# The turn between forward and backward of a decode block on one core: norms' sums gathered, do from a transposed Wo, loads and stores around it reordered

## The chip, the cores and the metric

The kernel runs on one core of one Trainium2 chip. The time is the device time of one execution in microseconds (us). The kernel before takes 1381.98 us, the median of 3 runs (1381.88 to 1382.74). A profiled execution gives, for each engine, what ran when and what it waited for. The engines are PE (matrix products), DVE (vector), ACT (scalar functions), POOL (here it only issues stores) and SP (issues loads); all transfers run on the core's 16 DMA engines.

## The reference

Forward and gradients of one block for a single token. Attention reads a cache of 32 heads, 8192 positions, 192 columns, in bf16; the gradients for K and V have the same size, so the kernel reads and writes some 570 MB.

```
h  = layernorm(x) * (1 + ca) + sa              # sa, ca, ga, sb, cb, gb from silu(c) @ w_mod
q  = h @ wq;  p = softmax(q k^T / sqrt(192));  o = p v
x  = x + ga * (o @ wo)
hb = layernorm(x) * (1 + cb) + sb
x1 = hb + (terms that shift one token, which are zero here)
x  = x + gb * (x1 + gelu(layernorm(x1) @ w3) @ w4)
grads with respect to x, k_cache, v_cache, wq, wo, w3, w4, c, w_mod
```

With p the softmax of a head and do the gradient that reaches its o: dV = p (outer) do, dP = V do, dS = p * (dP - p.dP), dK = dS (outer) q.

## The kernel before, in words

**Vectors as columns.** A vector of 640 is kept as a tile of 128 partitions by 5 columns. A layer norm needs sums over all of it: DVE adds along the columns, PE multiplies with a constant matrix (`negd_mat`, all -1/640, or `ones_mat_f`), which sums over the partitions and leaves the result on every one, and DVE goes on from PSUM. `ln_cols` (L152) does this twice, for the mean and then for the variance; `ln_bwd_cols` (L172) once.

**Forward.** For each head, K and V come in two tiles of 128 x 32 x 192 (1536 KB each). DVE multiplies K with q (L131, `prod`), PE adds up the scores (L359), ACT and DVE scale K by the exponentials (L392, L400, tile `EK`, four quarters a head) and PE makes products of V with the scaled K (L417 and L425, `fwd_kvA` and `fwd_kvB`, into banks A and B of PSUM) and the sum of the scaled K (L433, `fwd_kvK`, into `kb_ps`). The last column of `EK` carries the exponentials alone, so that the same product gives o. `fwd_keep` and `fwd_keepB` bring these banks to SBUF for the backward.

**The turn.** After head 31: o of the last pair, its product with Wo (L488), x1, the two norms, u = n2 @ w3 (L751), the gelu and its derivative, dn2 = du @ w3^T (L792), two norms backward, dao, do of the last pair (L1111), and do broadcast to all partitions (L190, `do_pb`). Only then can a dV be made. Beside it PE transposes w3 (60 blocks in 15 groups of 4, L646, with a cast by ACT each, L647) and the last pair's rows of Wo (L655), DVE makes the gradient of w4 (`dw4_some`, L782, with stores at L785) and the sums `d_g` (L524), and the four `fwd_kvK` of head 31 run.

**Backward.** Heads go from 31 down to 0. `bwd_dv` writes one dV tile: of its 32 rows ACT makes 20 (L948) and DVE 12 (L915), and POOL issues the store (L954). `bwd_mult` multiplies a V tile by do in place (L131), and PE adds it up (L930), which frees its slot for the next load. `bwd_dk` makes dK (DVE, L915; store at L969).

**Order.** The code's order is each engine's order: `pin_order` fixes it for PE, DVE and ACT, and SP and POOL issue in the order written, so an issue that waits for a slot holds back those behind it. V tiles in the backward, and batches of Wo, come through a ring of six slots (`ring_load`), of which a slot is loaded again when the tile in it is used up. K tiles, the weights w3 and w4 (`w_t`) and the output tiles share the pool `big` of five slots.

Of the kernel before, what the change touches and what calls it, by code (L numbers as in the profile page):

```python
# [20 lines left out]
def kernel(  # L21
# [43 lines left out]
    P = 128  # L65
# [75 lines left out]

    def col_sums(parts, n, name):
        ps = bank_c(name)
        nc.tensor.matmul(ps[:, 0:n], lhsT=ones_mat_f, rhs=parts, start=True, stop=True)
        return ps[:, 0:n]
# [6 lines left out]
    def ln_cols(x_c, pfx, fill=lambda k: None):  # L152
# [3 lines left out]
        fill(0)  # L156
# [4 lines left out]
        nc.vector.tensor_tensor_reduce(out=sq, in0=xc, in1=xc, scale=1.0 / D, scalar=0.0, op0=ALU.mult, op1=ALU.add, accum_out=s2)  # L161
# [5 lines left out]
        fill(1)  # L167
        nrm = ccol(NDC, pfx + "_n")
        nc.vector.tensor_scalar(out=nrm, in0=xc, scalar1=rstd[:, 0:1], scalar2=None, op0=ALU.mult)
        return nrm, rstd  # L170

    def ln_bwd_cols(dn, n, rstd, add_to, out, pfx, fill=lambda: None):  # L172
        s = ccol(2, pfx + "_s")
        nc.vector.reduce_sum(out=s[:, 0:1], in_=dn, axis=AX.X)
        jk = ccol(NDC, pfx + "_jk")
        nc.vector.tensor_tensor_reduce(out=jk, in0=dn, in1=n, scale=1.0, scalar=0.0, op0=ALU.mult, op1=ALU.add, accum_out=s[:, 1:2])
        m_ps = neg_means(s, 2, pfx + "_m")
        fill()
        t = ccol(NDC, pfx + "_t")
        mul(t, n, m_ps[:, 1:2].to_broadcast([P, NDC]))  # L180
        add(t, t, dn)
        add(t, t, m_ps[:, 0:1].to_broadcast([P, NDC]))
        stt(out, t, rstd[:, 0:1], add_to, ALU.mult, ALU.add)
# [54 lines left out]
    fpr_cm = tc.tile_pool(name="fprod", bufs=2)  # L238
    fpr = fpr_cm.__enter__()
# [36 lines left out]
    n0_c, r0 = ln_cols(x0_c, "ln0")  # L276
# [48 lines left out]

    def load_v(pool, h, t):
        tl = pool.tile([P, JH, DH], BF16, name="V_sb")
        nc.sync.dma_start(out=tl, in_=V_hd[h][:, t * JH : (t + 1) * JH, :])
        return tl
# [14 lines left out]
    def fwd_mult(h, t, st):  # L344
# [3 lines left out]
        prod = fpr.tile([P, JH, DH], BF16, name="prod")  # L348
# [126 lines left out]

    def fwd_o(hp):
        c0 = 3 * hp
        for h in (2 * hp, 2 * hp + 1):
            _, _, bp, ca_, cb_ = head_split(h)
            mul(o_col_f[:, ca_ : ca_ + 1], MA(h)[:, DH : DH + 1], rinv_bc[:, h : h + 1])  # L480
            mul(o_col_f[bp : bp + 64, cb_ : cb_ + 1], MB(hp)[bp : bp + 64, DH : DH + 1], rinv_bc[bp : bp + 64, h : h + 1])
        dve_copy(o_col_bf[:, c0 : c0 + 3], o_col_f[:, c0 : c0 + 3])
# [7 lines left out]
    def fwd_ao_add(hp, sm):  # L490
        if hp == 0:
            dve_copy(ao_c, sm[:, 408 : 408 + NDC])
        else:
            add(ao_c, ao_c, sm[:, 408 : 408 + NDC])

# [14 lines left out]

    def load_wt(k):
        w_t.append(flat(big_tile(f"w_t{k}")))
# [7 lines left out]
    def dg_some(f0, f1):  # L520
        jk_t = fpr.tile([P, JH, DH], BF16, name="prod").rearrange("p j d -> p (j d)")
        for f in range(f0, f1):
            jk = jk_t[:, f % 4 * D : (f % 4 + 1) * D]
            nc.vector.tensor_tensor_reduce(out=jk, in0=w4n(f, 0, D), in1=dbo_bc, scale=1.0, scalar=0.0, op0=ALU.mult, op1=ALU.add, accum_out=d_g[:, f : f + 1])  # L524
# [36 lines left out]
    for i in range(1, HQ + 2):  # L561
        if i == HQ + 1:
            nc.scalar.activation(out=warm, in_=eps_c, func=ACT.Sqrt)
# [6 lines left out]
        if i == HQ - 1:  # L570
            load_wt(0)
        fwd_load(i - 1, 1)
        if p:
            fwd_wo(i - 1, st[i - 1])
        if i == HQ:
            load_wt(1)
            load_wt(2)
        if pp:
# [6 lines left out]
        if i % 2 == 0 and i >= 4:  # L585
            fwd_ao((i - 4) // 2, st[i - 3]["wo"], st[i - 1]["sm"])
            fwd_ao_add((i - 4) // 2, st[i - 1]["sm"])
        if pp:
# [3 lines left out]
        if i > HQ:  # L592
            dg_some(9, NFC)
# [33 lines left out]
        if i == HQ:  # L627
            dg_some(0, 9)
    SB = [1024]
# [9 lines left out]
    w3T_next = [0]  # L639

    def w3T_some(n):
        for g in range(w3T_next[0], min(w3T_next[0] + n, NFC * NDC // 4)):
            t_ps = bank("s", 2, "t_ps", SB[0])
# [3 lines left out]
            nc.scalar.copy(out=w3T(4 * g, 4), in_=t_ps[:, 0:512])  # L647
        w3T_next[0] += n

    def woT_some(n):  # L650
        for g in range(woT_next[0], min(woT_next[0] + n, 4)):
            t_ps = bank("s", 2, "t_ps", SB[0])
            blks = range(4 * g, min(4 * g + 4, 3 * NDC))
            for k, blk in enumerate(blks):
                nc.tensor.matmul(t_ps[:, k * P : (k + 1) * P], lhsT=woT[:, blk * P : (blk + 1) * P], rhs=ident_bf, start=True, stop=True)  # L655
            nc.scalar.copy(out=woT[:, 512 * g : 512 * g + P * len(blks)], in_=t_ps[:, 0 : P * len(blks)])
        woT_next[0] += n

    woT = st[HQ - 1]["wo"].rearrange("p c r -> p (c r)")
    woT_next = [0]  # L660
    w3T_some(3)
    fwd_kvK(HQ - 1, 0, st[HQ - 1], True)
    fwd_kvK(HQ - 1, 1, st[HQ - 1], True)
    sm = bank_c("sm_ps")
    fwd_ao(HH - 1, st[HQ - 1]["wo"], sm)
    fwd_ao_add(HH - 1, sm)
    fwd_kvK(HQ - 1, 2, st[HQ - 1], True)
# [3 lines left out]
    fpr_cm.__exit__(None, None, None)  # L671
    psum_cm.__exit__(None, None, None)
    psum[0] = ctx.enter_context(tc.tile_pool(name="psum_b", bufs=1, space=bass.MemoryType.PSUM, reuse_waits="tile"))
    CB[0], SB[0] = 2, 512

    bv = ctx.enter_context(tc.tile_pool(name="bv", bufs=3, reuse_waits="tile"))
# [5 lines left out]
    V_b = {HS[0]: st[HS[0]]["V"]}  # L682
# [10 lines left out]
    def ring_load():  # L693
        while ring_n[0] < len(ring) and (ring_n[0] < NR - 2 or ring_key(ring_n[0] - NR) in freed):
            kind, k, t = ring[ring_n[0]]
            pool = bv if ring_n[0] % NR in (1, 2, 3) else fv
            ring_n[0] += 1
            if kind == "v":
# [5 lines left out]
            else:  # L704
                lo, n = PS[BATCHES[k][-1]], len(BATCHES[k])
                tl = pool.tile([P, JH, DH], BF16, name="V_sb").rearrange("p j d -> p (j d)")[:, 0 : 3 * n * D].rearrange("p (c r) -> p c r", r=D)
# [29 lines left out]
    x1_c = ccol(NDC, "x1_c")  # L736
    mul(x1_c, ao_c, ga)
    add(x1_c, x1_c, x0_c)
    n1_c, r1 = ln_cols(x1_c, "ln1", lambda k: w3T_some(k + 1))
    fwd_kvK(HQ - 1, 3, st[HQ - 1], True)  # L740
    hb_c = ccol(NDC, "hb_c")
    mul(hb_c, n1_c, cb1)
    add(hb_c, hb_c, sb)
    n2_c, r2 = ln_cols(hb_c, "ln2", lambda k: w3T_some(k + 1))
    nc.scalar.activation(out=warm, in_=eps_c, func=ACT.Exp)
    n2_bf = ccol(NDC, "n2_bf", BF16)
    dve_copy(n2_bf, n2_c)
    u_ps = bank("a")
    for f in range(NFC):
        for i in range(NDC):  # L750
            nc.tensor.matmul(u_ps[:, f : f + 1], lhsT=w3n(i, f * P, (f + 1) * P), rhs=n2_bf[:, i : i + 1], start=(i == 0), stop=(i == NDC - 1))  # L751
    w3T_some(2)
    u = ccol(NFC, "u")
    u2k = ccol(NFC, "u2k")
    inner = ccol(NFC, "inner")
    dve_copy(u, u_ps[:, 0:NFC])
    stt(u2k, u, GELU_K1, u, ALU.mult, ALU.mult)
    stt(inner, u2k, 1.0, u, ALU.add, ALU.mult)
    sg = ccol(NFC, "sg")
    nc.scalar.activation(out=sg, in_=inner, func=ACT.Exp, scale=-2.0 * GELU_K0)  # L760
    w3T_some(15)
    tb = ccol(NFC, "tb")
    affine(tb, u2k, 6.0 * GELU_K0, 2.0 * GELU_K0)
    mul(tb, tb, u)
    nc.vector.tensor_scalar(out=sg, in0=sg, scalar1=1.0, scalar2=None, op0=ALU.add)
    nc.vector.reciprocal(out=sg, in_=sg)
    deriv = ccol(NFC, "deriv")
    stt(deriv, sg, 1.0, tb, ALU.subtract, ALU.mult)
    stt(deriv, deriv, 1.0, sg, ALU.subtract, ALU.mult)
    du_bf = ccol(NFC, "du_bf", BF16)  # L770
    stt(du_bf, deriv, -1.0, d_g, ALU.mult, ALU.mult)
# [4 lines left out]
    dw4_n = [0]  # L776
    W4_O = (6, 3, 3)

    def dw4_some(n):
        for f in range(dw4_n[0], dw4_n[0] + n):  # L780
            tl, c0 = (w_t[2], f * D) if f < W4_O[0] else (w_t[1], W4_R * D + (f - W4_O[0]) * D)
            nc.vector.tensor_scalar(out=tl[:, c0 : c0 + D], in0=dbo_bc, scalar1=g_f[:, f : f + 1], scalar2=None, op0=ALU.mult)  # L782
            if f + 1 in (W4_O[0], W4_O[0] + W4_O[1], NFC):
                m = W4_O[0] if f < W4_O[0] else W4_O[1]
                st2.dma_start(out=out_7[(f + 1 - m) * P : (f + 1) * P, :].rearrange("(c p) r -> p c r", p=P), in_=tl[:, c0 - (m - 1) * D : c0 + D].rearrange("p (c r) -> p c r", r=D))  # L785
        dw4_n[0] += n

    dw4_some(6)
    dn2_ps = bank("b")
    for i in range(NDC):  # L790
        for f in range(NFC):
            nc.tensor.matmul(dn2_ps[:, i : i + 1], lhsT=w3T(f * NDC + i), rhs=du_bf[:, f : f + 1], start=(f == 0), stop=(f == NFC - 1))  # L792
    woT_some(1)
    bwd_pf_act(HS[0])
    dn2 = ccol(NDC, "dn2")
    dve_copy(dn2, dn2_ps[:, 0:NDC])
    dhb = ccol(NDC, "dhb")

    def lb2_fill():
        woT_some(2)  # L800
        dw4_some(2)

    ln_bwd_cols(dn2, n2_c, r2, dbo_c, dhb, "lb2", lb2_fill)

    def lb1_fill():
        woT_some(1)
        dw4_some(2)
        q_pb[PS[0]] = pair_bc(bsm, q_bf, PS[0], "q_pb")
# [392 lines left out]
```

## Time and profile before

| | |
|---|---|
| time, median of 3 runs | 1381.98 us (1381.88 to 1382.74) |
| the profiled execution: time, its span | 1382.37 us, 1380.6 us |
| mean granted TensorE clock | 0.785 |
| busy: DVE, ACT, PE, POOL | 78%, 69%, 62%, 8% |
| moved by DMA | 570.81 MB, mean 413 GB/s |
| read from and written to HBM | 343.08 MB, 225.91 MB |

The span goes from the first to the last instruction; the device time is 1.8 us longer. The DMA share of a stretch is the mean busy share of the 16 engines: at 1.0 something was under way on all of them all the time, at whatever rate. PEclk is the clock that PE was granted, as a share of its full clock. A line of the timeline gives the start, the time, the engine, the line of code, the operation with what it writes and reads, how many of a kind were merged, and in brackets the idle time before it and what ended it.

### The profile page before, as it was taken

The numbers are of one execution on the slowest core, as the hardware profiler recorded it, in microseconds if no ns is written. First come the engines' busy times: TensorE is split into PE (matmuls) and PEld (weight loads), VectorE is DVE, ScalarE is ACT, GpSimd is POOL, SyncE is SP. The second block draws the span as 40 slices with busy tenths as digits, with TensorE's granted clock in tenths as the row PEclk, the third lists the DMA queues.
The fourth block names the chain that finished last, engine by engine and source line by source line (L and its number), as shares of the span: only waits on it lengthen the run. The fifth ranks groups of instructions, "written<-read, shape, count | busy, mean of one in ns | idle before, by whom it ended". The sixth has DMA issues, their size and how long they took to land. (4 is left out here: it accounts for less than half of the span.)

```text
span 1380.6 us, 28080 instructions
## 1 busy us (share of the span) xinstructions
PE 854.9 (62%) x11519; PEld 672.0 (49%) x11519; DVE 1077.8 (78%) x1288; ACT 957.9 (69%) x2621; POOL 110.8 (8%) x202
## 2 busy tenths in 40 slices
PE   3699999999999999736636552344343343524341
PEld 3577777777777777625535541223122232313230
DVE  3688888888878786799988984876677678779793
ACT  1587787877878777786885596467665657558680
POOL 0000000000000000111111111111111111011011
PEclk9899999999999999666656566666666666666565
DMA  9999999999999999899999999999999999999997
GB/s 391 419 419 419 419 419 420 419 421 419 420 414 407 420 419 367 320 381 399 427 427 425 425 429 427 427 428 427 426 425 427 426 426 417 428 420 425 428 428 310
DMA packets 73167, 570.81 MB, mean 413 GB/s; under 512 B 6862, under 2 KB 19918, under 8 KB 32590
## 3 DMA queue, kind: packets, MB, share of 16 engines
q1 hardware_dynamic: 48736, 343.10, 60.3%
q0 software_dynamic: 24272, 225.92, 38.8%
q8 instruction: 90, 1.47, 0.4%
q14 instruction: 39, 0.32, 0.1%
q10 hardware_dynamic: 30, 0.00, 0.0%
HBM read 343.08 MB, written 225.91 MB: 412 GB/s over the span
## 5 line engine op out<-in xcount | busy, mean ns | idle before, releaser
L948 ACT ACTIVATE dV<-do_pb,PF 128x192 bf16<-128x192 bf16 x1260 | 439.3, 439 | 82.3 <-DMA out_dram<-dK 62.9
L930 PE MATMUL dP_ps<-V_sb,ident_bf 128*128 128x256 bf16 x1536 | 230.5, 325 | 235.4 <-DVE V_sb L131 235.4
L392 ACT ACTIVATE EK<-K_sb,E_f 128x192 bf16<-128x192 bf16 x1024 | 363.8, 442 | 14.2 <-PE kb_ps L433 8.1
L930 PEld LDWEIGHTS <-ident_bf 128*128 128x128 bf16 x1536 | 178.7, 117 | 287.0 <-issue 169.0
L131 DVE TENSOR_TENSOR prod<-K_sb,q_pb 128x6144 bf16<-128x6144 bf16 x64 | 214.6, 3354 | 37.1 <-DMA K_sb<-in_A_k_cache_dram 36.7
L915 DVE TENSOR_TENSOR dK<-dS,q_pb 128x6144 bf16<-128x6144 bf16 (+1 forms) x67 | 213.0, 3210 | 38.6 <-DMA out_dram<-dK 34.7
L417 PE MATMUL ps_a<-EK,V_sb 128*128 128x193 bf16 x2048 | 199.5, 250 | 28.3 <-DMA V_sb<-in_A_v_cache_dram 25.2
L131 DVE TENSOR_TENSOR V_sb<-V_sb,do_pb 128x6144 bf16<-128x6144 bf16 x64 | 211.8, 3350 | 5.8 <-DMA V_sb<-in_A_v_cache_dram 5.8
L417 PEld LDWEIGHTS <-V_sb 128*128 128x128 bf16 x2048 | 173.1, 99 | 48.9 <-DMA V_sb<-in_A_v_cache_dram 41.1
L400 DVE TENSOR_TENSOR EK<-K_sb,P2h 128x1536 bf16<-128x1536 bf16 x128 | 121.5, 950 | 0.0
L915 DVE TENSOR_TENSOR dV<-P2h,do_pb 128x2304 bf16<-128x2304 bf16 x63 | 83.7, 1356 | 43.8 <-DMA out_dram<-dV 40.5
L425 PE MATMUL ps_b<-EK,V_sb 128*64 128x193 bf16 x2048 | 111.5, 251 | 0.0
L359 PE MATMUL S_ps<-prod,ident_bf 64*64 64x256 bf16 x3072 | 99.9, 277 | 9.2 <-DVE prod L131 8.8
L359 PEld LDWEIGHTS <-ident_bf 64*64 64x64 bf16 x3072 | 83.5, 109 | 24.6 <-issue 23.8
L425 PEld LDWEIGHTS <-V_sb 128*64 128x64 bf16 x2048 | 83.6, 110 | 21.1 <-issue 21.1
L380 ACT ACTIVATE E_f<-sm_ps,negm 128x64 f32<-128x64 f32 x32 | 10.0, 314 | 84.1 <-DVE negm L378 84.1
L954 POOL DMA_DIRECT2D out_dram<-dV x63 | 33.7, 534 | 399.2 <-ACT dV L948 285.6
L433 PE MATMUL kb_ps<-EK,hot_bf 128*32 128x384 bf16 x1024 | 65.4, 333 | 0.0
L1020 PEld LDWEIGHTS <-ident_bf 128*128 128x128 bf16 x112 | 15.1, 135 | 93.9 <-issue 92.7
L984 ACT ACTIVATE wq_o<-wq_bc,ha_f 128x1536 bf16<-128x1536 bf16 x12 | 18.5, 1566 | 49.6 <-DMA out_dram<-wq_o 49.6
L194 ACT CAST do_pb<-bc_ps 128x384 bf16<-128x384 f32 x16 | 7.5, 469 | 65.0 <-PE bc_ps L190 65.0
L969 POOL DMA_DIRECT2D out_dram<-dK x67 | 37.0, 553 | 176.6 <-DVE dK L915 138.0
(247 smaller groups left out, 823.0 us busy)
## 6 DMA issues: line engine op xcount, KB each, us to landing
V_sb<-in_A_v_cache_dram SPq DMA_DIRECT2D x126, 1536.0 KB, 16.8
K_sb<-in_A_k_cache_dram SPq DMA_DIRECT2D x64, 1536.0 KB, 20.0
out_dram<-dV POOLq DMA_DIRECT2D x63, 1536.0 KB, 21.8
out_dram<-dK POOLq DMA_DIRECT2D x63, 1536.0 KB, 21.8
wq<-in_A_wq_dram SPq DMA_DIRECT2D x3, 2560.0 KB, 33.9
wo_t<-in_A_wo_dram SPq DMA_DIRECT2D x16, 480.0 KB, 19.9
out_dram<-dwo POOLq DMA_DIRECT2D x16, 480.0 KB, 19.2
wq<-in_A_wq_dram SPq DMA_DIRECT2D x4, 1920.0 KB, 35.9
```

The lines of the kernel that those rows point to most:

```text
L131: nc.vector.tensor_tensor(out=out, in0=a, in1=b, op=ALU.mult)
L359: nc.tensor.matmul(st["S_ps"][c0 : c0 + 64, r, t * JH : (t + 1) * JH, :], lhsT=ident_bf[64 * r : 64 * r + 64, 64 * r : 64 * r + 64], rhs=p ...
L392: nc.scalar.activation(out=EK[:, jj, 0:DH], in_=K_st[h, t][:, r * JQ + jj, :], func=ACT.Copy, scale=st["E_f"][:, j : j + 1])
L400: nc.vector.tensor_tensor(out=EK[:, NA:JQ, 0:DH].rearrange("p j (d r) -> p j d r", r=2), in0=K_st[h, t][:, r * JQ + NA : (r + 1) * JQ, :]. ...
L417: nc.tensor.matmul(st["A_ps"][:, 0 : DH + 1], lhsT=V_sb[:, r * JQ + jj, a0:a1], rhs=EK[:, jj, 0 : DH + 1], start=(q == 0 and jj == 0), sto ...
L425: nc.tensor.matmul(st["B_ps"][g : g + 64, 0 : DH + 1], lhsT=V_sb[:, r * JQ + jj, b0:b1], rhs=EK[:, jj, 0 : DH + 1], start=(q == 0 and jj < ...
L433: nc.tensor.matmul(kb_ps[g : g + 32, 0 : 2 * DH], lhsT=hot_bf[:, HQ - 1 - h : 2 * HQ - 1 - h], rhs=EK[:, jj : jj + 2, 0:DH], start=(h == 0 ...
L915: nc.vector.tensor_tensor(out=o.rearrange("p j (d r) -> p j d r", r=2), in0=pairs[:, :, None, :].to_broadcast([P, n, NP2, 2]), in1=vec.rea ...
L930: nc.tensor.matmul(bst[h]["dP_ps"][:, t * JH : (t + 1) * JH, :], lhsT=ident_bf, rhs=V_sb[:, :, k * DS : (k + 1) * DS], start=(k == 0), sto ...
L948: nc.scalar.activation(out=o[:, jj, :], in_=doh, func=ACT.Copy, scale=bst[h]["PF"][:, j0 + jj : j0 + jj + 1])
L954: st2.dma_start(out=dV_hd[h][:, j0 + r0 : j0 + r1, :], in_=o[:, r0:r1, :])
L969: st2.dma_start(out=dK_hd[h][:, j0 : j0 + n, :], in_=o[:, r0 : r0 + n, :])
```

## The change

- **Order of loads.** `load_wt(0)` (the first nine rows of blocks of w4) goes behind both V tiles of head 30. Both V tiles of head 29 are loaded ahead of the turn into the two slots that `prod` used; the ring now has three slots in `fv`, one in `bv` and these two.
- **Sums.** Seven of the twelve `d_g` products run before head 30's last V products, and the rest after head 31's softmax work; they write their unused result to spare columns of `w_t[1]`.
- **o of head 31** is taken from PSUM, without the copy, and only the last pair's product with Wo stands in the turn, in three parts, with a group of transposes between.
- **Norms.** The first norm takes its mean, its variance and the mean of hb from one product over three sums; the second only needs its variance, which is computed while u = hb @ w3 runs on the unscaled vector. Backward, four sums of dn2 and six constants prepared earlier give both norms with one product, and eight steps on DVE lead to dao.
- **do** no longer goes from columns to a broadcast: Wo's rows are transposed into `woT2`, and a product with dao repeated on all partitions gives do for all partitions at once, in two halves.
- **PE's order.** Six of the fifteen groups of transposes run before u, nine after it, with the four `fwd_kvK` of head 31 among them; all of it before dn2.
- **Start of the backward.** dV of head 31, then the first dV of head 30 (8 rows by ACT, 24 by DVE) before V's product of head 31, then the second. `dw4` leaves the turn for iterations 17 to 20 of the backward (three ACT copies each), and dw3 moves from 17 to 21 to 21 to 25.

Its core:

```diff
@@ forward loop
-        if i == HQ - 1:
-            load_wt(0)
         fwd_load(i - 1, 1)
         if p:
             fwd_wo(i - 1, st[i - 1])
+        if i == HQ - 1:
+            alloc_wt(0)
+            load_wt(0)
         if i == HQ:
             load_wt(1)
             load_wt(2)
+            V_b[HQ - 3] = [load_v(fpr, HQ - 3, t) for t in range(2)]
+            dg_some(0, 7)
...
@@ the turn
+    fwd_kvA(LH, 2, sl)
+    fwd_kvB(LH, 2, sl)
+    fwd_kvB(LH, 3, sl)
+    fwd_kvA(LH, 3, sl)
...
+    mul(o_col_bf[:, ca_ : ca_ + 1], sl["A_ps"][:, DH : DH + 1], rinv_bc[:, LH : LH + 1])
...
+    last_ao(0)
+    last_ao(1)
+    w3T_some(1)
+    last_ao(2)
...
+    mul(ta, ao_ps, ga)
+    nc.vector.scalar_tensor_tensor(out=xs, in0=ta, scalar=1.0, in1=x_pre, op0=ALU.mult, op1=ALU.add, accum_out=s3[:, 0:1])
+    dot(jk, xs, xs, s3[:, 1:2])
+    dot(jk, xs, cb1, s3[:, 2:3])
+    w3T_some(1)
+    fwd_keep(LH, sl)
+    w3T_some(1)
+    nc.tensor.matmul(m3, lhsT=negd_mat, rhs=s3, start=True, stop=True)
+    fwd_keepB(LH, sl)
...
+    u_mm(0, 4)
+    nc.tensor.matmul(tn[:, 8:9], lhsT=negd_mat, rhs=s1, start=True, stop=True)
+    u_mm(4, NFC)
...
+    w3T_some(4)
+    for q in range(2):
+        fwd_kvK(LH, q, sl, True)
+        w3T_some(1, (act_copy, dve_copy)[q])
...
+    for q in range(2, 4):
+        fwd_kvK(LH, q, sl, True)
+        w3T_some(1, (act_copy, dve_copy)[q - 2])
+    w3T_some(1)
...
+    dn2_ps = bank("b", name="dn2_ps")
...
+    nc.tensor.matmul(tn[:, 16:22], lhsT=negd_mat, rhs=cs, start=True, stop=True)
...
+            pool = (fv, bv, fpr, fpr, fv, fv)[ring_n[0] % NR]
...
+    woT_some(2)
+    bwd_pf_act(HS[0])
+    bwd_pf_act(HS[1])
...
-    dw4_some(6)
...
+    for k, w in enumerate((n2_c, cb1, cbn)):
+        dot(jk, dn2v, w, s4[:, k + 1 : k + 2])
+    nc.tensor.matmul(m4, lhsT=negd_mat, rhs=s4, start=True, stop=True)
+    woT_some(3)
...
+    stt(dao_bf, h1, md[:, 0:1], zd, ALU.mult, ALU.add)
...
+    for c0 in (DH, 0):
+        for j in range(NDC):
+            nc.tensor.matmul(do_ps[:, c0 : c0 + DH], lhsT=dao_bf[:, j : j + 1].to_broadcast([P, P]), rhs=woT2[:, j, c0 : c0 + DH], start=(j == 0), stop=(j == NDC - 1))
+        act_copy(do_pb[PS[0]][:, c0 : c0 + DH], do_ps[:, c0 : c0 + DH])
@@ start of the backward
-    do_pb[PS[0]] = pair_bc(bsm, do_bf, PS[0], "do_pb")
-    bcast_dao()
-    mid_mm()
-    bwd_dv(HS[0], 0, 0, 2, w_t[3].rearrange("p (j d) -> p j d", d=DH))
-    c_first = fin_c(PS[0], 1)
-    bwd_dv(HS[0], 1)
+    h2_mm()
+    bwd_dv(HS[0], 0, 0, 2, w_t[3].rearrange("p (j d) -> p j d", d=DH))
+    bwd_dv(HS[0], 1)
+    dve_copy(do_bf[:, 3 * PS[0] : 3 * PS[0] + 3], do_ps[:, 400:403])
+    bwd_dv(HS[1], 0, 8)
+    c_first = fin_c(PS[0], 1)
+    bcast_dao()
+    q_pb[PS[0]] = pair_bc(bsm, q_bf, PS[0], "q_pb")
+    act_copy(kb_sb, kb_ps[:, 0 : 2 * DH])
+    mid_mm()
+    bwd_mult(HS[0], 0)
+    ring_load()
+    bwd_dv(HS[1], 1)
+    bwd_mult(HS[0], 1)
```

## The prediction

> **What bounds the kernel now.** I read the page's row of slices first, then the table of windows around the turn, then the timelines of PE, DVE, SP and POOL there, and last the chain of waits.
>
> ```profile
> DMA  9999999999999999899999999999999999999997
> GB/s 391 419 419 419 419 419 420 419 421 419 420 414 407 420 419 367 320 381 399 427 427 425 425 429 427 427 428 427 426 425 427 426 426 417 428 420 425 428 428 310
> ```
>
> Nearly every slice of 34.5 us moves 420 to 428 GB/s; only those around the turn (520 to 640 us) fall to 320 to 399. The windows show the loss closer (columns: busy us of PE, PEld, DVE, ACT, POOL, then granted clock, DMA share, GB/s):
>
> ```profile
> 520.00:530.00 10.00, 9.51 (x197) 7.29 (x192) 9.10 (x16) 9.95 (x31) 0.00 (x0) 1.00 0.84 313
> 530.00:560.00 30.00, 26.36 (x384) 20.91 (x381) 18.59 (x58) 17.93 (x49) 0.00 (x0) 0.94 1.00 390
> 560.00:570.00 10.00, 8.73 (x165) 7.56 (x158) 5.21 (x28) 7.45 (x15) 0.00 (x0) 0.56 0.94 368
> 570.00:580.00 10.00, 8.56 (x126) 7.55 (x124) 8.22 (x29) 7.38 (x19) 3.06 (x4) 0.50 0.62 228
> 580.00:590.00 10.00, 6.08 (x41) 4.64 (x42) 9.95 (x9) 9.97 (x30) 1.09 (x2) 0.57 0.71 291
> 590.00:600.00 10.00, 3.11 (x28) 2.40 (x26) 9.79 (x16) 9.18 (x27) 1.60 (x3) 0.77 0.97 331
> 600.00:640.00 40.00, 15.84 (x104) 11.91 (x103) 38.74 (x58) 32.40 (x87) 5.82 (x10) 0.67 1.00 400
> ```
>
> From 600 us to the last store the DMA share stays at 1.00 to 1.01, and the last store lands 19 us after POOL's last issue, so work is queued to the end. The bytes don't change, so **the end moves by the change in the DMA engines' idle time**. From 560 to 600 they idle 0.6 + 3.8 + 2.9 + 0.3 = 7.6 us. Faster engines after 600 us are worth nothing. The turn's chain:
>
> ```profile
> 537.48 2.77 PE L417 MATMUL ps_a<-EK,V_sb 128*128 128x193 bf16 x16 [1.98 <-DMA V_sb<-in_A_v_cache_dram]
> 553.21 0.86 PE L425 MATMUL ps_b<-EK,V_sb 128*64 128x193 bf16 x16
> 568.20 2.03 PE L792 MATMUL ps_b<-du_bf,w_t 128*128 128x1 bf16 x60
> 567.53 0.17 DVE L140 SCALAR_TENSOR_TENSOR du_bf<-deriv,d_g 128x12 bf16<-128x12 f32 x1
> 576.28 3.43 DVE L915 TENSOR_TENSOR w_t<-P2h,do_pb 128x3072 bf16<-128x3072 bf16 x2 [0.52 <-ACT do_pb L194]
> 520.31 6.32 SPq L328 DMA_DIRECT2D V_sb<-in_A_v_cache_dram  x1
> 578.34 0.56 POOL L954 DMA_DIRECT2D out_dram<-w_t  x1 [1.53 <-DVE w_t L915]
> ```
>
> Head 31's V products end at 554.07 (553.21 + 0.86), du is ready at 567.70, the dn2 product runs 568.20 to 570.23, and the first dV starts at 576.28. The reads run out near 569.6; dw4's stores fill part of the hole.
>
> **The change, part by part.** E is the end of head 31's V products.
>
> *1. Order of loads.* w_t0 goes behind head 30's second V tile, which was free to go at 520.31 (its slot's last reader ended there) but was 6.32 us in issue behind w_t0's issue of 517.19. That cost PE 1.98 us of wait and a halved clock: 2.77 and 1.11 us for two groups that take 1.53 and 0.86 just after, 3.5 us in all. The V tile now leads. Two things limit the gain: head 31's second V tile, issued at 535.09, lands about 546 to 548 (estimate from its neighbour's 13.8 us), and the weights of w_t2 land at 552.4 (537.92 + 14.5) while a transpose of them now stands inside the chain. At best E comes 2.0 us earlier. At worst the long issue falls on head 31's first V tile (issued 527.37, landed 541.2, needed at 545) and E is 1.5 later. I take 1.5 earlier, nearer the row with the wait; E = 552.6.
>
> *2. Edits that cost nothing.* dg's first seven products (7 x 0.75 = 5.2 us) go into a DVE hole of 5.64 us before 542.23; without that cover they are 5.2 us on DVE before E. Head 29's two V tiles are loaded before the turn, but the DMA share from 546 to 558 is already 1.03, so this only changes which bytes go first. SP has nothing behind them but the slot waits of head 30's tiles. dw3's shift and dw4's twelve ACT copies (about 0.5 us each, from the 128x512 casts' 0.53 pitch) stand where the DMA share is 1.01.
>
> *3. From E to du.* o from PSUM 0.25; two thirds of Wo's product, one transpose group and the last third 0.35 + 0.31 + 0.1 (15 one-column products took 0.51, 8 transposes 0.62); four DVE steps at the 0.20 pitch of the norm's dependent steps 0.75; one trip through PE 0.54; a wait for ACT's copy of B, behind two casts, about 0.55; then five more DVE steps and hb's write 1.3: u's product starts at E + 4.15. It takes 1.74 plus 0.35 for the second norm's product inside it (E + 6.25). u to du: 0.6, the exponential 0.3, 1.05 more: du at E + 8.2, against E + 13.6 now. The table load (1.28) lies beside u's product.
>
> *4. What is late next: PE.* Nine of fifteen w3 transpose groups and four kb products moved behind u. A group took 0.51 at the granted clock 0.50 and 0.31 at 1.00; a kb product 0.42 at 1.00 (16 matmuls in 0.83), unseen at 0.50, so between 0.42 and 0.83; I take 0.75, nearer the doubling that the V products showed. All at 0.50: 9 x 0.51 + 4 x 0.75 = 7.6, dn2 starts at E + 13.85. All at 1.00: 4.5, with ACT's casts (0.53 each, behind the exponential) holding the two PSUM tiles a little: E + 11.0. Before it was E + 14.13. So of the 5.4 us won at du, 0.3 to 3.1 remain. I take E + 12.4, the middle: dn2 starts at 565.0 and ends at 567.0.
>
> The row on the clock is 0.50 from about 561.6 to 588, though PE was busy 93% of 563.3 to 570.2, and 1.00 returned only after 48 wide products (584.95 to 592). The Trainium skill, "TensorE: Matmul & The Clock Gate", Part 1, says half rate is the idle state and that one window of about 3.4 us of sustained activity brings the full clock back. By that rule the new, gapless run of transposes and kb products would go to full clock and dn2 would start at E + 11.0; by the row it might stay halved to E + 13.85. This trace bears the rule out only for wide products.
>
> *5. From dn2 to the first dV.* Now 576.28 - 570.23 = 6.05: two norms in series, do as columns, a cast, a broadcast, a copy. After: four sums and the product behind them, which queues on PE behind cs (0.5) and six Wo transposes (0.8), 1.95 in all; eight fused DVE steps, partly independent, 1.25; five 192-column products 0.7 and the copy 0.35 (estimates from 128-column broadcasts at 0.17 each and 128x384 casts at 0.48): 4.3. The first dV starts at 567.0 + 4.3 = 571.3, against 576.28, 5.0 earlier.
>
> *6. What DMA gets.* The reads end 0.8 earlier (568.8), by the 0.5 us idle of 534 to 542 and 0.24 of 560 to 562 that earlier slots fill. w_0, the Wo batch, waits for the kb products that read the EK tiles it overlays, about 562.5; the queue before it lasts to about 564.5. The first half dV is issued 2.06 after the first dV's start, and its bytes start about 1.8 later (share rises near 572 after the issue of 570.07): 575.2, so a gap of 6.4. Both halves run to 579.0. dV of head 31's second half needs 20 ACT writes (7.02), from 572.6 as ACT first copies do's other half: bytes at 581.7, a gap of 2.7. From there head 30's first dV (8 writes, 2.8) and the V loads, whose slots free with the products at about 586.5 against 589.50, follow without a hole. Idle: 9.1 against 7.6, **+1.5**: dw4's 1.97 MB, 5.3 us of DMA work that stood in the hole, is now in the full stretch. Against it, **-0.8** of idle before, and **-1.2** because the loads at 590 to 596, now alone in flight at 203 to 362 GB/s, will run beside queued stores (they lose 1.9 us against 424 GB/s; 0 to 1.9 can come back, I take two thirds). DVE's chain to head 31's last dK is 27.3 against 25.6 us, as 12 more rows of dV are on it; the queue covers that. Sum: -0.5 us.
>
> The profiled execution took 1382.37 (span 1380.6), 0.4 over the median of 1381.98; the difference is taken to the median: 1381.5.
>
> **Rivals.** *PE at full clock:* dn2 1.4 earlier still, do's products 0.4, E its full 2.0, slow loads all regained (0.7): -0.5 - 3.0 = -3.5, **1378.5**. For it: no gaps are left in PE's run. Against: 93% busy was not enough here. *PE is the gate, slower:* the transposes and kb products stay halved (+1.45), the long issue moves to head 31's tile so that E is not earlier (+1.5), nothing of the slow loads comes back (+1.2): +3.65, **1385.6**. It decides when dn2's first matmul starts after 567; then the hole that dw4 used to fill stays open. For it: the clock row and the 6.32 us issue. *It doesn't do what it says:* Wo's five casts (0.48 each, behind two P copies of 0.35) end after dao, and do waits 0.5 for them: **1382.0**.
>
> **How the numbers follow.** Forecast 0.40, full clock 0.30, gate 0.26, Wo's casts 0.04. 0.2% (2.8 us) is about what a measurement of this kernel can tell from no change: faster 0.30 (the full clock), same 0.44 (forecast and casts), slower 0.26. The range goes past both rivals by what is left in the bounds (E, the kb products, the stores' start): 1377.0 to 1387.0; the forecast's own is 1379.5 to 1384.
>
> **What would show it.** Right: V products of head 31 end at 552 to 553, du 8 us later, dn2 starts at 564 to 566, the first dV at 570 to 573, and DMA idles 6 to 7 us before it. Wrong: PE waits for a V tile at head 31 (step 1), dn2 starts where the last transposes end past 567 (step 4), or the DMA share after 600 falls below 1.0, which would break the rule that only idle time counts.

## The result and the profile after

| | before | after |
|---|---|---|
| median of the runs, us | 1382.33 (4 runs, 1381.88 to 1382.74) | 1400.57 (4 runs, 1396.51 to 1401.11) |
| ratio, 95% interval | | 1.0126 (1.0106 to 1.0145) |
| profiled execution / its span, us | 1382.37 / 1380.6 | 1400.24 / 1398.4 |

The changed kernel is 18.2 us slower. I had forecast 1381.5, with a range that ended at 1387.0. Both kernels move the same 570.81 MB. The page's rows of slices, after (34.96 us a slice):

```profile
DMA  9999999999999999588999999999999999999997
GB/s 393 417 420 419 418 419 421 419 421 419 420 409 418 409 406 376 235 345 342 425 428 424 426 429 428 427 429 426 427 426 425 425 422 422 423 413 428 427 429 295
```

Three slices are low, at 559 to 664 us: the hole of the turn is deeper (235 against 320), and the two slices behind it stay at 342 to 345, where the kernel before had 381 and 399. The windows show where. Columns as in the prediction: busy us of PE, PEld, DVE, ACT, POOL, then granted clock, DMA share, GB/s. First the kernel before:

```profile
560.00:600.00 40.00, 26.48 (x347) 22.16 (x340) 33.18 (x81) 33.98 (x89) 5.75 (x9) 0.60 0.81 304
600.00:640.00 40.00, 15.84 (x104) 11.91 (x103) 38.74 (x58) 32.40 (x87) 5.82 (x10) 0.67 1.00 400
640.00:680.00 40.00, 30.55 (x192) 26.23 (x191) 39.54 (x49) 29.62 (x81) 4.58 (x8) 0.62 1.01 426
```

The same windows of the changed kernel:

```profile
560.00:600.00 40.00, 25.35 (x336) 19.00 (x334) 26.87 (x80) 27.92 (x73) 2.68 (x5) 0.59 0.55 215
600.00:640.00 40.00, 10.98 (x85) 8.54 (x84) 35.84 (x53) 33.71 (x90) 4.66 (x9) 0.67 1.00 398
640.00:680.00 40.00, 30.65 (x196) 26.16 (x195) 39.49 (x51) 19.06 (x50) 4.33 (x8) 0.67 0.88 352
680.00:720.00 40.00, 25.82 (x152) 21.22 (x152) 39.29 (x59) 31.66 (x87) 5.17 (x10) 0.67 1.01 426
```

Read the last column as bytes: 40 us at 304 GB/s are 12.16 MB, at 215 they are 8.60. **The changed kernel is 3.56 MB behind after the turn, and loses another 2.96 MB between 640 and 680**; at the full stretch's 426 GB/s these are 8.4 and 6.9 us. With 0.2 us between, it is 15.5 us of transfer behind at 680, and it never catches up, since from there both run at 426. I call this number, MB not moved by a point divided by 426 GB/s, the **lag**. It was still 15.5 at 1200 us; 2.3 us more come after that and before the end (17.8 between the spans). Of these 1.3 us lie in the last 60 us (351 GB/s against 360 in the last 60 us of the kernel before); no instruction was found for them. A finer window of the changed kernel shows the second loss (the kernel before moves 426 GB/s there):

```profile
640.00:650.00 10.00, 7.49 (x50) 5.69 (x48) 9.83 (x18) 0.00 (x0) 1.83 (x3) 0.79 0.50 139
```

The timelines (start, duration, line, operation, and in brackets the idle time before and what ended it) answer to the rows that the prediction quoted. First three rows of the kernel before, from PE and SP:

```profile
584.95 7.13 PE L930 MATMUL dP_ps<-V_sb,ident_bf 128*128 128x256 bf16 x48 [3.88 <-DVE V_sb L131]
589.50 2.95 SPq L328 DMA_DIRECT2D V_sb<-in_A_v_cache_dram  x2
633.76 21.22 SPq L328 DMA_DIRECT2D V_sb<-in_A_v_cache_dram  x4
```

PE, after:

```profile
543.99 0.38 PE L473 MATMUL sm_ps<-rowsum,ones_mat_f 128*128 128x2 f32 x2 [1.96 <-DVE ao_c L134]
553.20 1.54 PE L419 MATMUL ps_a<-EK,V_sb 128*128 128x193 bf16 x16
570.95 1.64 PE L812 MATMUL dn_ps<-du_bf,w_t 128*128 128x1 bf16 x60
594.89 7.80 PE L1051 MATMUL dP_ps<-V_sb,ident_bf 128*128 128x256 bf16 x48
```

DVE, after:

```profile
564.47 0.17 DVE L140 SCALAR_TENSOR_TENSOR du_bf<-deriv,d_g 128x12 bf16<-128x12 f32 x1
574.19 0.46 DVE L875 CAST P2h<-PF 128x128 bf16<-128x128 f32 x2 [1.80 <-ACT PF L871]
578.89 3.43 DVE L1036 TENSOR_TENSOR w_t<-P2h,do_pb 128x3072 bf16<-128x3072 bf16 x2 [1.36 <-ACT do_pb L194]
602.73 0.69 DVE L1079 TENSOR_REDUCE dP<-dP_ps 128x64 f32<-128x512 f32 x1 [4.86 <-PE dP_ps L1051]
```

SP's issues, after:

```profile
527.47 8.71 SPq L330 DMA_DIRECT2D V_sb<-in_A_v_cache_dram  x2
570.32 0.38 SPq L852 DMA_DIRECT2D V_sb<-in_A_wo_dram  x1
600.10 2.95 SPq L330 DMA_DIRECT2D V_sb<-in_A_v_cache_dram  x2
644.72 21.10 SPq L330 DMA_DIRECT2D V_sb<-in_A_v_cache_dram  x4
```

du is 3.1 us earlier than before (564.64 against 567.70), as meant. But dn2 ends later (572.59 against 570.23), the first dV starts 2.6 later, head 31's dP sums 9.9 later (594.89 against 584.95), head 28's V loads go out 10.6 later (600.10 against 589.50) and the next four 11.0 later (644.72 against 633.76).

### The profile page after: what moved, and what is told of

The parts are those of the page before. It is cut to its first block, busy times and chain, and to the rows that moved or that the text cites. A ratio compares the mean times of both kernels' runs of the same rounds, so it can differ in the third digit from the quotient of the medians.

```text
span 1398.4 us, 28097 instructions
## 1 busy us (share of the span) xinstructions
PE 849.0 (61%) x11512; PEld 667.9 (48%) x11512; DVE 1081.3 (77%) x1317; ACT 962.2 (69%) x2622; POOL 111.7 (8%) x203
## 2 busy tenths in 40 slices
DMA packets 73183, 570.81 MB, mean 408 GB/s; under 512 B 6878, under 2 KB 19934, under 8 KB 32606
## 4 chain that ended last, share of the span: by engine, by line
DMA 46%; PE 20%; DVE 18%; issue 7%; ACT 6%; SPq 2%; POOL 0%; another core or an unknown queue 0%; POOLq 0%; DVEq 0%; ACTq 0%
DMA V_sb<-in_A_v_cache_dram 15%; DMA out_dram<-dV 12%; PE ps_a L419 7%; DMA out_dram<-dK 6%; DVE dK L1036 5%; DVE V_sb L131 5%; PE ps_b L427 4%; DMA wq<-in_A_wq_dram 4%; PE S_ps L361 3%; ACT dV L1069 3%; DMA K_sb<-in_A_k_cache_dram 2%; DMA out_dram<-wq_o 2%; DVE dV L1036 2%; DMA out_dram<-dw 2%; PE kb_ps L435 2%
## 5 line engine op out<-in xcount | busy, mean ns | idle before, releaser
L1036 DVE TENSOR_TENSOR dV<-P2h,do_pb 128x2304 bf16<-128x2304 bf16 (+1 forms) x63 | 84.9, 1374 | 46.4 <-DMA out_dram<-dV 43.8
```

What stands on the lines that cost most here:

```text
L1036: nc.vector.tensor_tensor(out=o.rearrange("p j (d r) -> p j d r", r=2), in0=pairs[:, :, None, :].to_broadcast([P, n, NP2, 2]), in1=vec.rea ...
```

## The experiments

Times of one group were taken beside runs of the kernel before on the same chip; its median there lay between 1382.3 and 1383.2, so each kernel is given by its distance to it. The lag is worked out as above, from 520 to 720 us, against the kernel before's profile; it stands for the one profiled execution of a kernel, the distance for the medians. The 95% interval reaches 1.2 to 2.7 us to either side of a distance, so a difference of less than about 2 to 3 us between two changed kernels is not clear of noise unless the text says otherwise.

| kernel | median, us | ratio to before, 95% | distance, us | lag at 720, us |
|---|---|---|---|---|
| changed kernel | 1400.57 | 1.0106 to 1.0145 | +18.2 | 15.6 |
| e1, no dw4 | 1393.36 | 1.0061 to 1.0091 | +10.8 | 15.2, less 4.2 |
| e2, before without dw4 | 1383.87 | 1.0002 to 1.0022 | +1.3 | 5.4, less 4.2 |
| e3, TensorE's order | 1396.12 | 1.0075 to 1.0113 | +13.6 | 11.4 |
| e4, sums first | 1397.50 | 1.0087 to 1.0117 | +15.0 | 13.0 |
| p1, before, delay at head 30 | 1387.92 | 1.0021 to 1.0045 | +4.7 | 4.6 |
| p2, before, delay at head 25 | 1383.27 | 0.9991 to 1.0010 | +0.1 | 0.8 |
| x5, dw4 at heads 30 and 29 | 1399.51 | 1.0093 to 1.0132 | +16.3 | 13.3 |
| x8, five edits | 1399.80 | 1.0106 to 1.0140 | +16.6 | 13.4 |
| e9, kb products first | 1398.39 | 1.0099 to 1.0129 | +15.5 | 13.3 |
| e10, dw4 in the turn | 1393.93 | 1.0066 to 1.0105 | +11.0 | 9.6 |
| e12, e11 without dw4 in the turn | 1391.66 | 1.0052 to 1.0082 | +8.8 | 7.0 |
| e11, five other edits | 1386.80 | 1.0020 to 1.0040 | +3.9 | 2.7 |
| b1, before, dw4 late | 1387.52 | 1.0018 to 1.0039 | +4.4 | 3.5 |
| b2, before, new order of dV and V | 1386.98 | 1.0014 to 1.0035 | +3.8 | 2.3 |
| e14, e11 and five d_g ahead | 1385.65 | 1.0010 to 1.0029 | +2.5 | 2.3 |
| e13, e14 and the old order | 1384.36 | 0.9994 to 1.0013 | +1.2 | -0.7 |
| c2, before, job_mid later | 1380.45 | 0.9969 to 0.9987 | -2.1 | -0.8 |

### Parts of the change, one at a time

The expectations call DVE VectorE, PE TensorE and ACT ScalarE. My first theory after the result, **A**: until head 29's V products VectorE paces the reads; that place came 10.64 us later (the rows below, kernel before and after) and is carried to the end one for one, and dw4's stores, now in the full stretch, cost about 5 us more.

```profile
625.71 6.62 DVE L131 TENSOR_TENSOR V_sb<-V_sb,do_pb 128x6144 bf16<-128x6144 bf16 x2
636.35 6.62 DVE L131 TENSOR_TENSOR V_sb<-V_sb,do_pb 128x6144 bf16<-128x6144 bf16 x2
```

**e1** leaves out dw4's products and all its stores but one row block (1.8 MB less, 4.2 us of transfer); **e2** does the same to the kernel before.

```
-    for k in range(NFC // 3):
-        J1[1 + HH + k].append(lambda k=k: job_dw4(k))
+    st2.dma_start(out=out_7[0:P, :], in_=dbo_bc)
```

> The changed kernel without the gradient of w4 (its products and stores are left out but for one row block, so this output is incomplete). Theory A (the time after about 640 us is DMA work that is left by then, and dw4's 1.97 MB was moved into it): 5.3 us less than the changed kernel, about 1395. Rival B (the loss is all in the late first dV and the waits behind it; the later stores of dw4 find room): no change, 1400.

> The kernel before, without the gradient of w4 (left out but for one row block). Theory A: its stores stood in a stretch where the DMA engines idle anyway, so it is worth 0 to 1.5 us at most (DVE's 4.6 us lie mostly beside PE): 1381 to 1382. Rival B': DMA bytes count wherever they stand: 5.3 us less, 1377.

e1 came out 7.4 us nearer to the kernel before; in the kernel before leaving dw4 out gained nothing (1.3 more). dw4 was free in the old hole and is paid for in its new place. The 7.4 us are more than the 4.2 us of transfer that e1 leaves out; 4.6 of them show in the lag (15.6 against 15.2 less 4.2), the rest comes after 1200 us, in the part that has no explanation.

**e3** moves the broadcasts of dao and q, the copy of kb (the sums of head 31's scaled K) and mid_mm (16 small products with kb) from behind head 30's first dV to ahead of the first dV:

```
     h2_mm()
+    bcast_dao()
+    q_pb[PS[0]] = pair_bc(bsm, q_bf, PS[0], "q_pb")
+    act_copy(kb_sb, kb_ps[:, 0 : 2 * DH])
+    mid_mm()
     bwd_dv(HS[0], 0, 0, 2, w_t[3].rearrange("p (j d) -> p j d", d=DH))
```

> The changed kernel with the broadcast of dao, q's broadcast, the copy of kb and its products put ahead of the first dV, as in the kernel before, so that the sums of V's product no longer queue on PE behind copies that ACT makes only after 28 rows of dV. Theory A (DVE's place at head 29's V products sets when loads go on): DVE's wait of 4.86 us for dP goes, ACT's dV starts about 2 us later: 3 to 5 us less than the changed kernel, 1396. Rival B (only the first dV's start counts): 0 to 1 us less or somewhat more, 1400.

Measured 4.6 less. In the changed kernel these small products stand on PE ahead of the V sums and wait for ACT, which writes 28 rows of dV (580.12 to 589.80) before it copies dao. In e3 that wait is gone, and VectorE no longer waits for dP:

```profile
597.83 0.68 DVE L1079 TENSOR_REDUCE dP<-dP_ps 128x64 f32<-128x512 f32 x1
```

**e4** moves the P casts, g_f and g_bf from ahead of the four sums of dn2 to behind dao:

```
+    dve_copy(m0d, m4[:, 0:1])
     bwd_pf_dve(HS[0])
     bwd_pf_dve(HS[1])
     ...
-    dve_copy(m0d, m4[:, 0:1])
```

> The changed kernel with the two casts of P (P2h) and the cast of g moved on DVE from ahead of the four sums of dn2 to behind dao. Theory A: the sums start 2.2 us earlier, as they no longer wait for ACT's copies of Wo's transposes and P, and the first dV comes 1.5 to 2 us earlier: 1398.5. Rival C (Wo's own casts on ACT gate do): the first dV moves by under 0.7 us, 1400.

Measured 3.2 less, near the edge of the noise: from dn2's end to the first dV it took 4.6 us (571.65 to 576.21) instead of 6.3. Up to here theory A fits: in e3 and e4 head 29's place moved by -4.2 and -2.75 us and the spans by -4.7 and -3.0. (0.94 of e4's 2.75 us were there at dn2, 570.01 against 570.95, ahead of its edit.)

### Does VectorE's place set the end, or DMA's bytes?

**p1** and **p2** put twelve dummy VectorE instructions into the kernel before, at head 30 or at head 25:

```
             dve_copy(dmod_bf[:, 2 * NDC : 6 * NDC], dmod_c[:, 2 * NDC : 6 * NDC])
+            for _ in range(12):
+                nc.vector.tensor_tensor(out=kb_sb, in0=kb_sb, in1=kb_sb, op=ALU.max)
```

> The kernel before the change, with twelve more VectorE instructions (element-wise maximum of a dead 128x384 float tile with itself, an estimated 0.4 us each, 5 us in all) behind head 30's small column work, just ahead of head 29's V products. Nothing is left out. Theory A (until head 29's V products VectorE paces the reads, and its place there is carried to the end one for one): the end moves by the added time, so about 1387.5. Rival B, the rule of my prediction (from 600 us to the end the DMA queue is the bound and covers VectorE): 1382.5, no change.

> The same twelve VectorE instructions in the kernel before the change, but five heads later (behind head 25), where the trace shows DMA fully busy. Theory A: the queue covers it there, 1382.5 to 1383.5. Rival C (VectorE paces the whole backward half): about 1387.5. Rival B: 1382.5 as well; B and A differ only in the other run.

The delay cost 4.7 us at head 30, where it starts at 624 us, and nothing at head 25, at 742 us. (It was 7.0 us long, 0.58 each; VectorE was 1.25 earlier in p1's execution, which leaves 5.7, so the cost is not quite one for one.) The windows of p1, then of p2:

```profile
600.00:640.00 40.00, 12.65 (x84) 9.51 (x84) 38.54 (x55) 32.40 (x87) 4.86 (x9) 0.61 0.86 355
640.00:680.00 40.00, 28.13 (x175) 24.22 (x174) 39.53 (x49) 23.51 (x63) 5.01 (x9) 0.64 1.00 404
```

```profile
600.00:640.00 40.00, 14.41 (x99) 10.87 (x97) 38.78 (x57) 33.13 (x89) 6.30 (x11) 0.67 1.00 396
640.00:680.00 40.00, 31.26 (x193) 26.73 (x194) 39.51 (x48) 28.37 (x77) 4.58 (x8) 0.62 1.00 423
```

p1's DMA ran dry for about as long as VectorE came later (a share of 0.86 over 40 us), p2's did not. So my rule that faster or slower engines after 600 us count for nothing is wrong at 624 us and right at 742 us. Where between the two it turns was not measured, and x8 below has a dry stretch at 680 to 720.

**x5** moves the four dw4 jobs to heads 30 and 29; **x8** adds e3's and e4's edits, job_mid (the column work for the output x and for the gradients of sa to gb) at head 25 instead of 30, and all d_g reductions behind head 31's other work.

```
-        J1[1 + HH + k].append(lambda k=k: job_dw4(k))
+        J1[1 + k // 2].append(lambda k=k: job_dw4(k))
```

> The changed kernel with the four dw4 jobs moved from heads 14 to 11 to heads 30 and 29, two each, so that their stores fall into the stretch at 630 to 650 us where DMA runs dry. Nothing is left out. Leaving the stores out gained 7.2 us. Theory A: most of that comes back, 1394 to 1396. Rival D (ScalarE's 36 us of other work in heads 30 and 29 pushes the dV rows and so the dV stores back): 1399 to 1402.

> The changed kernel with five edits at once: the broadcasts, q_pb, kb_sb and mid_mm ahead of the first dV (alone -4.5), P2h and g behind dao (alone -3.1), dw4 at heads 30 and 29, the first seven d_g reductions back behind head 31's other VectorE work (PE's 1.96 us wait and the halved clock go, an estimated -1.5), and job_mid moved from head 30 to head 25 (an estimated -4). Theory A: the place of head 29's V products comes from 636.4 to about 624, and the time to 1380 to 1384, about that of the kernel before. Rival B (the end is the queue's, the edits act each for another reason): 1388 to 1393.

Both miss theory A by far. x5 lies in rival D's range. x8 misses rival B's range as well, and it is the end of theory A: head 29's V products start at 627.81, only 2.1 later than in the kernel before, DMA is full from 600 to 680, and the time is still 16.6 us over. A row of x8 from ACT, one from DVE, and one window:

```profile
670.08 2.27 ACT L1121 ACTIVATE dw<-dbo_bc,g_f 128x640 bf16<-128x640 bf16 x3 [15.64 <-DMA out_dram<-dwo]
```

```profile
673.37 0.23 DVE L874 CAST P2h<-PF 128x128 bf16<-128x128 f32 x1 [14.90 <-ACT PF L870]
```

```profile
680.00:720.00 40.00, 24.50 (x146) 20.96 (x146) 39.36 (x50) 33.62 (x90) 5.90 (x10) 0.61 0.97 385
```

The jobs share two store buffers. dw4's job has to wait until a dwo store has gone through the full queue (15.64 us, and 13.14 in x5); ACT's order is fixed, so the next head's P waits behind it, VectorE stands for 14.9 us, and a dry stretch follows at 680 to 720 (385 GB/s, 3.9 us). In addition nothing had been done about the hole: 201 GB/s from 560 to 600.

That leaves theory **L**, the ledger: what DMA doesn't move while it is dry, in the hole or later, has to be moved behind it at full rate, wherever it was lost. VectorE's place is one of the things that make it dry. (x5's profiled execution, its slowest, loses once more near the end: 363 GB/s from 1210 to 1240 against 419, another 3.9 us. Its span ends 19.0 us later at a lag of 13.3.)

### Undoing parts together

**e9** puts head 31's four kb products ahead of and among the first late w3 groups; **e10** puts dw4 back on VectorE in the turn; **e11** is e3, e4, e9, e10 and job_mid at head 25; **e12** is e11 without e10.

```
-    w3T_some(4)
-    for q in range(2):
+    for q in range(4):
         fwd_kvK(LH, q, sl, True)
-        w3T_some(1, (act_copy, dve_copy)[q])
+        w3T_some(1)
...
+    dw4_some(4)
     psum_cm.__exit__(None, None, None)
...
     bwd_dv(HS[0], 0, 0, 2, w_t[3].rearrange("p (j d) -> p j d", d=DH))
+    dw4_some(3)
+    dw4_some(5)
```

> The changed kernel with head 31's four kb products ahead of and among the first of the nine late w3 transpose groups (where TensorE waits for ScalarE's casts), instead of behind the fourth. Nothing is left out. In the changed kernel the Wo batch w0 waits for the last of them until 570.3 us. Theory L (the end is DMA's bytes: what is not moved in the hole of 560 to 600 or in the dry stretch of 640 to 650 has to be moved behind it at full rate; the changed kernel is 8.4 us of transfer behind at 600, 15.3 at 650 and 15.5 at 1200): the load starts near 566, dn2 ends 1 to 2 us sooner, the time falls by 3 to 5, to 1395.5 to 1397.5. Theory A (only VectorE's place at head 29 counts): -1 to -2, 1398.5 to 1399.5. Rival (the transposes are later by what the kb products take): 1400 to 1402.

> The changed kernel with dw4's twelve products back on VectorE in the turn: four behind dao, in its 1.4 us wait for do_pb, eight behind the first dV; the stores leave at about 580 to 587, in the hole. Nothing is left out. Theory L: 1.97 MB more in the hole (4.6 us at 425 GB/s; leaving the stores out gained 7.2) against 2.4 us of later VectorE work: -3 to -5, 1395.5 to 1397.5. Rival R (as when dw4 was moved to heads 30 and 29, the reads fall dry later instead): 1399 to 1402.

> The changed kernel with five edits at once: the broadcasts and mid_mm ahead of the first dV (alone -4.5), P2h and g behind dao (alone -3.1), the kb products first, dw4 back in the turn, and job_mid moved from head 30 to head 25. Theory L: about the sum, 1381 to 1387, and a lag in bytes against the kernel before of 0 to 4 us from 650 on. Rival R (each gain is given back in a later dry stretch, as in the first run of many edits): 1390 or more, with the lag at 600 small and a new loss at 640 to 720.

> The same without dw4 back in the turn (its stores stay at heads 14 to 11). Theory L: 4 to 7 us above the one with it, 1386 to 1392. Rival R: no more than 2 us above it, or below it.

e10 gives 7.2, more than L expected, e11 14.3 and e12 4.9 less than e11, both as expected. e9 gives 2.7, between L's 3 to 5 and A's 1 to 2, and not clear of noise, and not by L's way. Its Wo batch did leave 4.9 us sooner:

```profile
565.44 0.38 SPq L852 DMA_DIRECT2D V_sb<-in_A_wo_dram  x1
```

But the lag at 600 hardly moved (7.8 against 8.4): 332 GB/s instead of 239 from 560 to 570, and 55 instead of 149 from 570 to 580. A read that is issued earlier fills nothing if no read behind it can be issued earlier too. dn2 does start earlier (568.82 against 570.95), but 1.76 of these 2.13 us were there at E (552.98 against 554.74), ahead of the edit. So what the edit itself gained, if anything, is not shown.

The windows of e11 at the hole and at the dry stretch:

```profile
560.00:600.00 40.00, 28.33 (x343) 21.25 (x342) 31.65 (x95) 28.05 (x74) 5.29 (x8) 0.61 0.76 285
640.00:680.00 40.00, 28.53 (x173) 24.61 (x174) 39.37 (x55) 26.47 (x72) 4.02 (x7) 0.62 1.00 417
```

### Parts alone on the kernel before, and the last microseconds

**b1** is the kernel before with dw4 as the change's four ACT jobs at heads 14 to 11. **b2** is the kernel before with the change's order of dV and V products. **e14** is e11 with five instead of seven d_g reductions ahead of ao_c, **e13** is e14 with the old order.

```
     bwd_dv(HS[0], 1)
+    bwd_pf(HS[1])
+    bwd_dv(HS[1], 0, 8)
+    bwd_mult(HS[0], 0)
+    ring_load()
+    bwd_dv(HS[1], 1)
+    bwd_mult(HS[0], 1)
```

> One part of the change alone, on the kernel before: dw4's twelve products leave the turn and become the change's four jobs on ScalarE at heads 14 to 11, with dw3 four heads later. Nothing is left out. Theory L: without dw4's products and stores the kernel before was 5.5 us of transfer behind from 640 to 1000 us and ended at the same time only because 4.3 us of transfer were missing; with the stores late the end comes 5 to 7 us later, 1388 to 1390. Rival (dw4's place costs nothing by itself, only together with the changed kernel's longer hole): 1382 to 1384.

> One part of the change alone, on the kernel before: its order of head 31's and head 30's dV and head 31's V products (both dV of head 31, the first of head 30 with eight rows on ScalarE, then V product, dV, V product); the broadcasts stay ahead of the first dV. Theory L: the second V tile is freed some 5 us later and head 28's loads with it, against one dV store that leaves some 7 us earlier: +1 to +4, 1384 to 1387. Rival W (the writes fill the hole, the order is the part that gains): 1380 to 1382.

> The kernel of five edits, with two more: the order of dV and V products of the kernel before, and only five d_g reductions ahead of ao_c instead of seven (the other two join the five behind). Theory L: the V tiles are freed some 5 us earlier and head 31's output 1.6 us earlier, 3 to 5 below the kernel of five edits, 1382 to 1384. Rival W: no better than the next run.

> The kernel of five edits with only five d_g reductions ahead of ao_c instead of seven: TensorE's 1.96 us wait for ao_c shrinks to 0.4 and its clock stays full, so head 31's V products end some 1.6 us earlier, all of the turn with them. Theory L: -1 to -2, 1385 to 1386. Rival (the chain behind E waits for VectorE's last d_g instead): 1386.5 to 1387.5.

dw4's new place costs 4.4 us by itself, somewhat under the 5 to 7 expected. The turn did not get shorter without its products: from dn2's end to the first dV it takes 6.05 us with and without them. The new order costs 3.8. In the hole b2 moves more (321 GB/s against 304: head 30's first dV store is issued at 585.94 instead of 591.49, though 1.7 us of that come from an earlier first dV, ahead of the edit); the loss comes later, at 600 to 640, because V tiles are freed later (head 28's loads go out at 593.82 instead of 589.50):

```profile
600.00:640.00 40.00, 14.28 (x98) 10.83 (x97) 38.92 (x51) 31.37 (x85) 6.35 (x11) 0.66 0.95 372
```

On e14 the old order gives 1.3 back; ten runs of each, on the same chip, tell the two apart. The 1.4 between e11 and e14 is within the noise. e14's E is 1.6 earlier (552.20 against 553.81), but PE then waits 0.87 us for w_t at 553.44, so du is 0.65 earlier, and nothing of that reaches the first dV (576.42 against 576.18).

e13 is level with the kernel before (0.9994 to 1.0013). It holds job_mid at head 25, which is no part of the change and gains 2.1 us alone (c2 below). So what is left of the change in it, each norm's sums in one product, o from PSUM and Wo transposed, shows no gain, and may cost something. That its first dV is 1.9 us earlier than the kernel before's (574.41) is no gain of the change either: e14 has the same code up to there and starts it at 576.42. In e13's execution PE's clock came back to 1.00 at 565.0 for 6.8 us, in e14's it stayed at 0.50 beyond the first dV.

**c2** follows from the ledger: the kernel before has a small dry stretch too, at 630 to 640.

```
             mid_cols()
-            job_mid()
-            dve_copy(dmod_bf[:, 2 * NDC : 6 * NDC], dmod_c[:, 2 * NDC : 6 * NDC])
+            dve_copy(h2_f, mid_ps["h2"][:, 0:NDC])
+        if i == 6:
+            job_mid()
+            dve_copy(dmod_bf[:, 2 * NDC : 6 * NDC], dmod_c[:, 2 * NDC : 6 * NDC])
```

> The kernel before the change with job_mid (2.1 us of VectorE's work and one trip through TensorE) moved from head 30 to head 25; h2 is copied out of PSUM at head 30. Nothing is left out. Theory L: in the kernel before, DMA moves only 330 GB/s from 630 to 640 us, 2.2 us of transfer short of a full stretch, because head 28's and 27's loads wait for VectorE at head 29; with VectorE 2 us earlier there, 1 to 2 us come back: 1381 to 1382. Rival B (nothing after 600 us matters): no change, 1383.

Measured 0.9978 (0.9969 to 0.9987), 2.1 us less, the fastest kernel of this study. The window in the kernel before, then in c2:

```profile
630.00:640.00 10.00, 7.18 (x51) 5.64 (x49) 9.79 (x19) 6.92 (x17) 1.84 (x3) 0.84 0.94 330
```

```profile
630.00:640.00 10.00, 7.70 (x55) 6.24 (x52) 9.76 (x20) 6.96 (x17) 1.83 (x3) 0.84 1.00 375
```

## Why the prediction was wrong

**The step that failed is number 6, "What DMA gets".** Its rule, that the end moves by what DMA doesn't do while it is dry, held when counted in bytes: the lag gives each distance within 3.2 us, over a spread of 20. What failed is its count. It predicted 9.1 us of idle time in the hole against 7.6 (a share of 0.81 over 40 us); it was 18.0 (0.55). And it took all after 600 us as covered: "the queue covers that". There VectorE ran late enough that DMA was dry at 640 to 650 (a share of 0.50), another 6.9 us of transfer. p1 shows that this cover is not there at head 30, p2 that it is five heads later. The prediction had named a share below 1.0 after 600 us as a sign of being wrong, and it came. The DMA share of 1.00 from 600 to 640, on which I rested the rule, hid it: at that share the kernel before moved 400 GB/s, and 330 in its last quarter, where the V loads had just run out. "From 600 us to the last store the DMA share stays at 1.00 to 1.01" was a wrong reading: from 630 to 640 it was 0.94. And dw4's 1.97 MB are 4.6 us at 426 GB/s, not 5.3.

By the steps:

*1, order of loads.* Right as far as it goes. PE no longer waits for head 30's V tile and reaches the Wo product of the pair before 2.8 us earlier (538.89 against 541.67). The long issue went to head 31's tiles (8.71 us for two), but PE waits for neither. E came at 554.74 instead of 552.6 by step 2. (A sum in it is off: 535.09 and 13.8 make 548.9, not 546 to 548.)

*2, edits that cost nothing.* The seven d_g products did not fit their hole. It begins only when w_t0 lands (537.83) and closes at 542.23, and they run at a pitch of 0.87, not 0.75, so they end at 543.8. PE waits 1.96 us for ao_c behind them, and the clock is at 0.50 from 545.2 to 548.6, where three groups take 1.91, 1.50 and 2.04 us instead of 1.53, 0.86 and 1.53. That used up the 2.8 us of step 1. In e9's execution the clock stayed at 1.00 after a wait of 2.25, and E was 552.98; with five products instead of seven (e14) it was 552.20. dw4 belongs to step 6, and the growth of job_mid (ten more steps, 2.0 us on VectorE at head 30) I did not price at all.

*3, from E to du.* 9.9 us instead of 8.2; still much less than the 13.6 before. Ahead of u PE waits 0.61, 1.43 and 0.94 us for ACT's casts of the transposes.

*4, what is late next.* Named rightly, sized wrongly: dn2 starts at E + 16.2, outside my bounds of 11.0 to 13.85. u's product ends at E + 7.5 instead of 6.25, and from there to dn2 it takes 8.7 us where 7.6 was the bound at half clock. In these PE waits another 2.3 us for ACT's casts (1.36, 0.73 and 0.23), which I had priced as "a little". The clock counted as well: it was at 0.50 for most of the run. These two windows of the changed kernel show its return:

```profile
568.00:569.00 1.00, 1.00 (x16) 0.40 (x12) 0.00 (x0) 0.34 (x1) 0.00 (x0) 0.50 0.00 0
569.00:570.00 1.00, 1.00 (x21) 0.43 (x20) 0.84 (x3) 0.13 (x1) 0.00 (x0) 0.95 0.00 0
```

The last gap on PE ended at 565.83, and the full clock came at about 569.1, 3.3 us later and 1.9 before dn2. The Trainium skill, "TensorE: Matmul & The Clock Gate", Part 1, which asks for some 3.4 us of sustained activity, agrees with this. It doesn't settle e14: there PE ran without a gap from 558.3 to 566.4 and the clock stayed at 0.50. What the clock was worth can be read from e13 and e14, which have the same code up to the first dV: with the full clock from 565.0 (e13) dn2 starts 1.37 us earlier and the first dV 2.01. As 0.39 of both were there before the clock came back, this leaves 1.0 and 1.6 us for the clock.

*5, from dn2 to the first dV.* 6.3 instead of 4.3. The P casts stand ahead of the four sums and wait 1.80 us for ACT; with them behind dao it is 4.6 (e4).

*6.* The Wo batch left at 570.32 instead of 562.5, but by e9 no gain of leaving earlier is shown. dw4's missing stores are the largest part: 7.2 us by e10, 4.9 by e12 against e11, 4.4 alone on the kernel before. Next come the small products that wait on PE behind ACT's rows (4.6, e3), which I had not seen, and the order of dV and V products (3.8 alone, 1.3 in e14), of which I had priced only twelve rows of dV: from the first dV to head 31's last dK it took 31.6 us, not 27.3. The parts overlap, so they don't sum; taken back together, with job_mid moved, they bring the time to the kernel before's (e13).

The rival "PE is the gate" named its condition rightly (dn2 after 567), and the clock was at 0.50 for most of the run as it said, but it put its price at 3.65 us, a fifth of what came. What I had held against a loss, that queued work hides a late engine, was never tested against the row that bears on it: when each load is issued, and what it waits for.

## What to carry to other kernels

Where DMA is the bound, keep the ledger in bytes and not in busy shares: take the MB moved by a point from the windows, before and after, and divide the difference by the full rate. Then ask of every engine that runs late whether the queue still holds work; the answer is where the next loads are issued and which tile's last reader they wait for. Work that fills a hole (here dw4's stores) is free only there, and a job moved into an earlier head must not share its few buffers with stores that are already queued, or its engine stops, and with it all that stands behind in its order.

## What I had not expected of the hardware

- At a DMA share of 1.00 to 1.02 the rate still ranged from about 375 to 431 GB/s over windows of 10 us or more (c2 from 630 to 640, the kernel before from 710 to 720). The share alone doesn't show a loss of a tenth.
- The same 128x640 reduction on VectorE takes 0.75 us from one to the next with its product written over four column ranges in turn, and 0.87 with all of them on one range. Whether the range is the reason no run separates.
- Two executions of the same code differ by 2.0 us at the first dV, 1.6 of it after the clock came back in one of them (e13 and e14). In the changed kernel the clock's changes in the turn stand at 545.2, 548.6, 558.9, 569.1 and 575.9 us, 3.4 us or a multiple of it apart, so where a gap falls between such points may decide; no run separates that.
- A 7 us delay of VectorE cost 4.7 us at head 30 and 0.1 us five heads later, with the same instructions.
